# Narrower scores for the two short groups, 71 memory columns, and memory V turned by DMA, in a two-part kernel on one core

## The chip, the cores and the metric

The kernel runs on one core of a Trainium2 chip. The metric is device time in microseconds (us) of one execution; medians are quoted. The granted clock is the share of full TensorE speed that the trace records; all runs below have state fast with a mean of 0.997 to 1.000, so none has to be set aside as slow. To turn a tile means to transpose it. "The trace" is the record of one profiled execution, and its span is some 1.7 us shorter than the measured time.

Engine names: PE is the matrix engine, PEld its weight loads, DVE the vector engine, ACT the scalar engine, POOL the general one, SP the engine whose queue issues most transfers.

## The reference, cut

Part A is a state-space layer, part B a transformer layer with a recurrent memory; their results stand side by side. The change touches B alone:

```python
# B: x (1, 2048, 1024), mem0 (1, 8, 1024), 32 heads of 128, segments of 32 tokens
mem = mem0
for s in range(64):
    h = concat([mem, x[:, 32*s:32*s+32]])            # 8 memory + 32 tokens
    q, k, v = h @ Wq, h @ Wk, h @ Wv                 # per head
    p = softmax(mask(q @ k.T * 128**-0.5))           # memory rows see all, tokens are causal
    o = (p @ v) @ Wo
    mem = o[:, :8]                                   # memory of the next segment
    outs.append(o[:, 8:])
```

Taken literally, this is a chain of 64 steps. The kernel guesses the memory of each segment (from the mean of the segment), computes all segments at once, and checks the guess at the end: each recomputed memory row has to lie within 2^-8 of the guess in relative norm. If not, a general path (a loop over the 64 segments) runs. With these inputs it never does.

## The kernel before, the parts that matter

Three segments of 32 tokens and one memory column of each make a group of 99 columns; there are 22 groups. The first holds two segments and seven rows of the first memory, the last holds two segments: these are the two short groups. The memory columns stand behind the tokens in one tile, 73 of them (7 + 66, some of them never used).

```python
NTL = 3 * NG; NMX = 7; NM = NTL + NMX                # 66 + 7 = 73 memory columns
XMAIN = 1920; XE = T + NM                            # short pass of q and k: 2121 - 1920 = 201 columns
...
def v_mem(self, hb, w=None):                         # V of the memory columns, four heads a block
    ...                                              # 32 matmuls of 73 columns, copied to vm
    for h in range(4):
        k.PE.transpose(pt[0:NM, h*128:(h+1)*128], vm[:, h, :], k.ident[:])
    ...
    k.SP.dma_start(self.vx[hb][64:64 + NMX, :], sv[0:NMX, :])
    k.SP.dma_start(self.vt[hb][:], sv[NMX:NM, :])    # one store to the table of memory rows
...
def att_front(self, hp, u):                          # scores of two groups and two heads
    for gg in range(2):
        g0 = (2 * u + gg) * GP
        for hh in range(2):
            PE.matmul(s[:, gg, hh, 0:GW], kt[:, hh, g0:g0+128], qt[:, hh, g0:g0+GW], ...)   # GW = 99
    k.S.activation(e[:], s[...], ACT.Exp, ...)       # on ACT
    k.G.tensor_tensor(m[...], e[:], mask, ALU.mult)  # on POOL
...
LEAD = 10                                            # steps of the q/k projections ahead of the attention
```

The first V tile of the attention is loaded (`b_v<-b_vx`) from the tables that `v_mem` stores to, on SP's queue, behind those stores. After the last output store comes the branch on the check's flag.

## Time and profile before

| | before |
|---|---|
| time, median of 3 runs | 1247.11 us (1246.69 to 1247.39) |
| PE busy, of the span | 1234.2 of 1245.3 us |
| waits of PE that the table of waits lists (gaps of 0.1 us are left out) | 1.3 us |
| first score matmul / first product with V / last matmul start at | 486.6 / 492.2 / 1239.0 us |
| from the last matmul's start to the end | 6.25 us |

The page begins with the busy time of each engine, its share of the span and its instructions; its part on the chain of work that ended last names the engines that the chain ran through:

```profile
...
PE 1234.2 (99%) x8270; PEld 662.5 (53%) x8342; DVE 667.7 (54%) x1250; ACT 263.4 (21%) x631; POOL 275.8 (22%) x407
...
PE 99%; issue 0%; DVE 0%
...
```

The table of waits of PE gives line, tile and what was waited for, then the total in us, the count, and the longest:

```profile
...
PE psR L64 <- DVE hpb L105: 1.3, 1, 1.3
```

The table of stretches gives, for each stretch (us from the start), its length, then the busy time and instructions of PE, PEld, DVE, ACT and POOL, the granted clock, and the share and rate of the transfers. These are the start, the two parts of the attention, and the end:

```profile
...
0.00:20.00 20.00, 18.62 (x136) 11.02 (x138) 8.13 (x30) 6.97 (x11) 12.48 (x82) 1.00 1.06 261
487.00:700.00 213.00, 213.00 (x1653) 127.60 (x1652) 134.08 (x342) 41.90 (x142) 61.19 (x70) 1.00 0.55 138
700.00:1018.00 318.00, 317.89 (x2466) 190.42 (x2465) 199.01 (x512) 61.66 (x210) 91.36 (x105) 1.00 0.49 116
1235.00:1246.00 11.00, 4.28 (x40) 3.60 (x37) 0.42 (x1) 0.38 (x1) 0.00 (x0) 0.81 0.06 16
...
```

PE is busy without a gap in the attention; no other engine is near its limit. A group of instructions is shown as line, engine, operation, out<-in, shapes, count | busy us, mean ns of one | idle time before:

```profile
...
L64 PE MATMUL psS<-b_q,b_k 128*128 128x99 bf16 x704 | 59.9, 208 | 0.0
...
L64 PE MATMUL psP<-b_xe,b_wq 128*128 128x201 bf16 x256 | 24.8, 250 | 0.1
...
L64 PE MATMUL psP<-b_xe,b_wv 128*128 128x73 bf16 x256 | 10.0, 197 | 0.0
L64 PE MATMUL psS<-b_ogT,b_wog 128*128 128x64 bf16 x256 | 8.8, 193 | 0.0
...
L64 PE MATMUL psP<-b_omT,t 128*128 128x73 bf16 x128 | 4.5, 197 | 0.0
...
L64 PE MATMUL psP<-ident,b_vm 128*73 128x128 bf16 x32 | 3.1, 219 | 0.0
...
```

The mean ns of one matmul is a latency, and matmuls overlap, so it doesn't price a column. The interval from start to start does: 44.2 ns at 99 columns where the latency is 208.

The first V load on SP's queue and the first product with V on PE (start, length, engine, instruction):

```profile
...
465.02 0.27 SPq L64 DMA_DIRECT2D b_vx<-b_vst  x1
465.34 0.29 SPq L64 DMA_DIRECT2D b_vt<-b_vst  x1
465.73 0.26 SPq L64 DMA_DIRECT2D b_v<-b_vt  x1
466.03 16.42 SPq L64 DMA_DIRECT2D b_v<-b_vx  x2
...
```
```profile
...
486.64 0.34 PE L64 MATMUL psS<-b_q,b_k 128*128 128x99 bf16 x4
...
491.85 0.34 PE L64 MATMUL psS<-b_q,b_k 128*128 128x99 bf16 x4
492.16 0.50 PE L64 MATMUL psO<-b_v,b_m 128*128 128x129 bf16 x6
...
```

And the longest wait of SP on itself, behind the last branch:

```profile
...
SPq L1156 <- SPq L1156: 2.8, 1, 2.8
...
```

### The profile page before, as it was taken

To read this page: it belongs to the slowest core of one execution; us is meant where nothing else is said; L and a number is where in the kernel's file an instruction comes from. 1 tells how busy PE (TensorE), PEld (TensorE's weight loads), DVE (VectorE), ACT (ScalarE), POOL (GpSimd) and SP (SyncE) were. 2 spreads that over 40 slices of the span, in tenths; PEclk is the share of its full clock that TensorE was granted. 3 is DMA by queue.
4 is the path that set the end of the run, shared out by engine and by line. 5 is a ranking of instruction groups with operands and counts; after the bars stand their busy time and mean duration, and the time that the engine had idled before them with its cause. 6 is when DMAs were issued, how large, how long until landed. Compare 5 with 4: busy or idle time off the path is not lost.

```text
span 1245.3 us, 20124 instructions
## 1 busy us (share of the span) xinstructions
PE 1234.2 (99%) x8270; PEld 662.5 (53%) x8342; DVE 667.7 (54%) x1250; ACT 263.4 (21%) x631; POOL 275.8 (22%) x407
## 2 busy tenths in 40 slices
PE   9999999999999999999999999999999999999998
PEld 5444444444455555556666656555665554446444
DVE  4688899998711124666666666666666641001000
ACT  5344444443310000211112111111211110000000
POOL 4111331212332321322222222222222220000000
PEclk9999999999999999999999999999999999999999
DMA  9965444554898734664454545545553379407000
GB/s 248 272 191 147 131 135 127 144 155 107 242 322 248 249 116 95 196 170 124 96 145 108 144 108 120 132 92 121 120 142 92 65 211 230 107 18 153 17 26 19
DMA packets 316246, 176.83 MB, mean 142 GB/s; under 512 B 138874, under 2 KB 301550, under 8 KB 316150
## 3 DMA queue, kind: packets, MB, share of 16 engines
q1 hardware_dynamic: 294054, 147.95, 47.8%
q10 hardware_dynamic: 21072, 24.38, 5.9%
q0 software_dynamic: 1024, 3.17, 0.7%
q8 instruction: 66, 1.08, 0.4%
q14 instruction: 30, 0.25, 0.1%
HBM read 89.14 MB, written 53.17 MB: 114 GB/s over the span
## 4 chain that ended last, share of the span: by engine, by line
PE 99%; issue 0%; DVE 0%
PE psP L64 82%; PE psU L64 9%; PE psS L64 3%; PE psO L64 2%; PE psR L64 2%; DVE b_xe L91 0%; DVE b_ost L91 0%; DVE a_n L962 0%; DVE hpb L105 0%; DVE ones L102 0%
## 5 line engine op out<-in xcount | busy, mean ns | idle before, releaser
L64 PE MATMUL psP<-b_xe,b_wq 128*128 128x480 bf16 (+1 forms) x1280 | 247.7, 343 | 0.1
L64 PE MATMUL psP<-b_xe,b_wk 128*128 128x480 bf16 (+1 forms) x1280 | 247.7, 343 | 0.0
L64 PE MATMUL psP<-b_wv,b_xe 128*128 128x512 bf16 (+2 forms) x1033 | 223.4, 372 | 0.8
L644 POOL TENSOR_TENSOR b_m<-b_e,maskB 99x396 bf16<-99x396 bf16 x160 | 139.8, 874 | 338.5 <-ACT b_e L641 338.5
L641 ACT ACTIVATE b_e<-psS 99x396 bf16<-99x396 f32 x176 | 88.2, 501 | 536.7 <-PE psS L64 533.4
L64 PEld LDWEIGHTS <-b_wk 128*128 128x128 bf16 x1280 | 119.4, 98 | 94.2
L64 PEld LDWEIGHTS <-b_wq 128*128 128x128 bf16 x1280 | 118.7, 98 | 87.7
L64 PEld LDWEIGHTS <-b_xe 128*128 128x128 bf16 x1056 | 101.8, 98 | 119.1 <-DVE b_xe L91 0.2
L91 DVE CAST b_k<-psP 128x480 bf16<-128x480 f32 (+1 forms) x192 | 97.4, 528 | 100.9 <-PE psP L64 100.9
L91 DVE CAST b_q<-psP 128x480 bf16<-128x480 f32 (+1 forms) x192 | 97.4, 528 | 93.1 <-PE psP L64 91.5
L64 PEld LDWEIGHTS <-b_ol 128*128 128x128 bf16 x864 | 84.3, 98 | 94.4
L64 PE MATMUL psU<-a_xT,a_bt 128*128 128x512 bf16 x493 | 113.9, 379 | 1.1
L64 PE MATMUL psP<-t,a_hl 128*128 128x512 bf16 x496 | 112.1, 379 | 0.8
L91 DVE CAST b_ost<-psP 128x512 bf16<-128x512 f32 (+1 forms) x17 | 11.5, 676 | 177.4 <-PE psP L64 176.3
L64 PE MATMUL psP<-wo,b_ol 128*128 128x512 bf16 (+1 forms) x440 | 91.9, 364 | 0.4
L64 PE MATMUL psP<-t,b_ol 128*128 128x512 bf16 x408 | 91.7, 379 | 0.4
L280 POOL TENSOR_SCALAR a_tt<-a_pr,a_tabf 128x1 f32<-128x1 f32 x48 | 34.1, 710 | 243.2 <-DVE a_pr L275 243.2
L661 DVE TENSOR_TENSOR b_ob<-psO,b_accR 99x384 bf16<-99x384 f32 x160 | 85.9, 553 | 2.4 <-DVE b_accR L660 0.4
L89 ACT ACTIVATE b_vst<-psP 128x512 bf16<-128x512 f32 x126 | 71.9, 589 | 71.3 <-PE psP L64 59.9
L267 DVE TENSOR_TENSOR a_pr<-psU,a_tabf 128x2048 f32<-128x2048 f32 x32 | 73.0, 2282 | 15.7 <-PE psU L64 14.0
L64 PEld LDWEIGHTS <-a_bt 128*128 128x128 bf16 x512 | 49.2, 98 | 57.6
L64 PEld LDWEIGHTS <-a_hl 128*128 128x128 bf16 x512 | 49.0, 98 | 56.7
(200 smaller groups left out, 962.7 us busy)
## 6 DMA issues: line engine op xcount, KB each, us to landing
b_v<-b_vx SPq DMA_DIRECT2D x16, 1122.0 KB
b_wv<-in_B_Wv_dram SPq DMA_DIRECT2D x16, 1024.0 KB
b_vx<-b_vst ACTq DMA_DIRECT2D x24, 544.0 KB
b_on<-b_ob SPq DMA_DIRECT2D x15, 720.0 KB
a_hs<-a_h SPq DMA_DIRECT2D x32, 256.0 KB
b_wog<-in_B_Wo_dram SPq DMA_DIRECT2D x4, 2048.0 KB
b_wq<-in_B_Wq_dram SPq DMA_DIRECT2D x16, 512.0 KB
b_wk<-in_B_Wk_dram SPq DMA_DIRECT2D x16, 512.0 KB
```

What stands on the lines that cost most here:

```text
L64: r = f(*a, **kw)
L89: self.S.activation(out, in_, ACT.Copy)
L91: self.V.tensor_copy(out, in_)
L267: V.tensor_tensor(pr[:], u[:].unsqueeze(1).to_broadcast([128, 2, 2, TB]), view(t3, [[TB + 1, 2], [TB + 1, 2], [1, TB]]), ALU.mult)
L280: G.tensor_scalar(tt[:, j:j + 1], w[:, j, TB - 1:TB], t3[:, 1, TB:TB + 1], None, ALU.mult)
L641: k.S.activation(e[:], s[0:GW, :, :, 0:GW], ACT.Exp, scale=float(E) ** -0.5, accum_out=self.accE[0:GW, i:i + 1])
L644: k.G.tensor_tensor(m[0:GW, 0:4 * GP].rearrange("p (a b q) -> p a b q", a=2, b=2)[:, :, :, 0:GW], e[:], mask[0:GW, :, :].unsqueeze(2).to_b ...
L661: V.tensor_tensor(self.ob[:, b0:b0 + n, :], o[0:GW, 0:n, 0:E], r.unsqueeze(2).to_broadcast([GW, n, E]), ALU.mult)
```

## The change

Its intent is to take columns off PE, which bounds the kernel. The unused memory columns go (71 instead of 73), the scores of the two short groups are computed on 73 and 65 columns, the guess on 63 and the check on 70, and memory V of six of the eight head blocks is turned by DMA, through HBM, and not by PE. Cut to its core (the masks, the order of the check's rows and the fills are left out):

```diff
-NM = NTL + NMX
+NT4 = NMX + 4
+NM = NMX + NSEG                      # 71
+Q0 = 64 + NMX + 2                    # 73: first group
+QZ = 65                              # last group
+NO = NMX + 3 + NTL - 6               # 70: rows of the check
...
+    def store_t(self, hb, s):
+        for r0, n, i in ((0, 2, NMX), (NTL - 3, 2, NMX + 2), (3, NTL - 6, NT4)):
+            self.k.SP.dma_start(self.vt[hb][r0:r0 + n, :]..., s[i:i + n, :, :])
...
+        if hb > 1:
+            k.V.memset(vm[:, :, NM:128], 0.0)
+            k.SP.dma_start(self.vmt[hb][:], vm[:].rearrange("p h n -> p (h n)"))
+            yield
+            ...
+            for h in range(4):
+                k.SP.dma_start_transpose(s[:, h, 0:E], self.vmt[hb][:, h * 128:(h + 1) * 128])
+            yield
+            k.SP.dma_start(self.vx[hb][64:64 + NMX, :]..., s[0:NMX, :, 0:EW])
+            self.store_t(hb, s[:, :, 0:EW])
...
-        k.SP.dma_start(self.vt[hb][:], sv[NMX:NM, :])
+        self.store_t(hb, st[:, 0, :, :])
...
+            n = Q0 if u + gg == 0 else QZ if u + gg == NU else GW
             for hh in range(2):
-                PE.matmul(s[:, gg, hh, 0:GW], kt[:, hh, g0:g0 + 128], qt[:, hh, g0:g0 + GW], ...)
+                PE.matmul(s[:, gg, hh, 0:n], kt[:, hh, g0:g0 + 128], qt[:, hh, g0:g0 + n], ...)
...                                   # exp and mask: two parts in the first and last step of a head pair
-        self.gx = c.tile([128, KC, NM], BF16, name="b_gx")
+        self.gx = c.tile([128, KC, NO], BF16, name="b_gx")
-        self.accE = c.tile([128, HP * NU], FP32, name="b_accE")
+        self.accE = c.tile([128, HP * (NU + 2)], FP32, name="b_accE")
+    k.maskZ = k.cst.tile([128, GW], BF16, name="maskZ")
```

More of the change, by code (lines that the diff above doesn't have):

```diff
@@ L117, in masks @@
     k.maskB = k.cst.tile([128, 2, GW], BF16, name="maskB")
+    k.maskZ = k.cst.tile([128, GW], BF16, name="maskZ")
+    G.memset(k.maskZ[:], 0.0)
     G.memset(k.maskA[:], 0.0)
@@ L120, in masks @@
     t = slice(GX, GW)
-    for m, ns in ((k.maskA[:, 0, :], 2), (k.maskA[:, 1, :], 3), (k.maskB[:, 0, :], 3), (k.maskB[:, 1, :], 3)):
+    for m, ns, c0 in ((k.maskA[:, 0, :], 2, Q0 - 2), (k.maskA[:, 1, :], 3, GX), (k.maskB[:, 0, :], 3, GX), (k.maskB[:, 1, :], 3, GX),
+                      (k.maskZ[:], 2, QZ - 1)):
         for j in range(ns):
@@ L126, in masks @@
                             pattern=[[1, 32]], channel_multiplier=-1)
-            G.memset(m[r, GX + j:GX + j + 1], 1.0)
+            if c0 != QZ - 1 or j == 0:
+                G.memset(m[r, c0 + j:c0 + j + 1], 1.0)
         if ns == 3:
@@ L134, in masks @@
                             pattern=[[1, 3]], channel_multiplier=-1)
-    m = k.maskA[:, 0, :]
+    for a, b, n in ((0, 64, 2), (QZ - 1, QZ, 1)):
+        v = k.maskZ[t, a:b].rearrange("p (j q) -> p j q", j=n)
+        G.memset(v, 8.0)
+        G.affine_select(out=v, in_=v, compare_op=ALU.is_equal, fill=0.0, base=0, pattern=[[1, n], [0, (b - a) // n]],
+                        channel_multiplier=-1)
+    m, c0 = k.maskA[:, 0, :], Q0 - 2
     G.memset(m[0:32, 64:64 + NMX], 1.0)
@@ L139, in masks @@
     G.memset(m[64:64 + NMX, 64:64 + NMX], 1.0)
-    G.memset(m[64:64 + NMX, GX:GX + 1], 1.0)
-    for a, b in ((32, 64), (GX + 1, GX + 2)):
+    G.memset(m[64:64 + NMX, c0:c0 + 1], 1.0)
+    for a, b in ((32, 64), (c0 + 1, c0 + 2)):
         G.memset(m[t, a:b], 8.0)
@@ L146, in masks @@
     G.memset(m[GX:GX + 1, 0:32], 1.0)
-    G.memset(m[GX:GX + 1, 64:64 + NMX], 1.0)
-    G.memset(m[GX:GX + 1, GX:GX + 1], 1.0)
-    G.memset(m[0:1, 64 + NMX:GX], 1.0)
-    G.memset(m[0:1, GX + 2:GX + 3], 1.0)
+    G.memset(m[GX:GX + 1, 64:64 + NMX + 1], 1.0)
 class PartA:
@@ L344, in __init__ @@
         self.vt = [k.drp.tile([NTL, 4 * EW], BF16, name=f"b_vt{i}") for i in range(HB)]
+        self.vmt = [k.drp.tile([E, 512], BF16, name=f"b_vmt{i}") for i in range(HB)]
         self.on = [k.drp.tile([T, 1024], BF16, name=f"b_on{i}") for i in range(4)]
@@ L378, in fill @@
         k.V.memset(z[:], 0.0)
+        one = tmp.tile([2, 4 * EW], BF16, name="b_one", bufs=1)
+        k.V.memset(one[:], 1.0)
         for hb in range(HB):
@@ L381, in fill @@
             k.SP.dma_start(self.vx[hb][T + 32:NSLOT, :], z[0:32, :])
+            k.SP.dma_start(self.vt[hb].rearrange("(g j) n -> g j n", j=3)[0:NG:NG - 1, 2, :], one[:])
         for q in range(4):
-            k.SP.dma_start(self.tn[q][NM:NR, 0:4 * EW], z[0:NR - NM, :])
-            k.SP.dma_start(self.tn[q][NM:NR, 1024 - 4 * EW:1024], z[0:NR - NM, :])
+            k.SP.dma_start(self.tn[q][NO:NR, 0:4 * EW], z[0:NR - NO, :])
+            k.SP.dma_start(self.tn[q][NO:NR, 1024 - 4 * EW:1024], z[0:NR - NO, :])
     def load_x(self, q):
@@ L506, in og @@
             for c in range(KC):
-                mm = k.PE.matmul(p[:, h * NSEG:(h + 1) * NSEG], w[:, c, h * 128:(h + 1) * 128], self.xbar[:, c, :], start=(c == 0), stop=(c == KC - 1))
+                mm = k.PE.matmul(p[:, h * NSEG:h * NSEG + NSEG - 1], w[:, c, h * 128:(h + 1) * 128], self.xbar[:, c, 0:NSEG - 1], start=(c == 0), stop=(c == KC - 1))
                 if late and h == 0 and c == 0:
                     k.tc.keep_in_program_order(mm)
-        k.copy("s" if late else "v", self.ogT[:, hb * 4:(hb + 1) * 4, :], p[:, 0:4 * NSEG].rearrange("p (h s) -> p h s", h=4))
+        k.copy("s" if late else "v", self.ogT[:, hb * 4:(hb + 1) * 4, 0:NSEG - 1],
+               p[:, 0:4 * NSEG].rearrange("p (h s) -> p h s", h=4)[:, :, 0:NSEG - 1])
     def load_wog(self, q, pool):
@@ L520, in guess @@
         pg = k.ps("S")
+        NS = NSEG - 1
         for q in range(4):
@@ L525, in guess @@
                 for h in range(H):
-                    PE.matmul(pg[:, c * NSEG:(c + 1) * NSEG], wo[:, h, dc * 128:(dc + 1) * 128], self.ogT[:, h, :], start=(h == 0), stop=(h == H - 1))
+                    PE.matmul(pg[:, c * NSEG:c * NSEG + NS], wo[:, h, dc * 128:(dc + 1) * 128], self.ogT[:, h, 0:NS], start=(h == 0), stop=(h == H - 1))
                 yield
@@ L530, in guess @@
         V.tensor_copy(m[:, :, NMX + 1:NMX + 2], pv[:, :, 0:1])
-        V.tensor_copy(m[:, :, NMX + 3:NM], pv[:, :, 1:NSEG])
+        V.tensor_copy(m[:, :, NMX + 2:NT4], pv[:, :, NS - 2:NS])
+        V.tensor_copy(m[:, :, NT4:NM], pv[:, :, 1:NS - 2])
         gx = self.gx
-        V.tensor_copy(gx[:, :, 0:2], pv[:, :, 0:2])
-        V.tensor_copy(gx[:, :, 2:NTL - 1], pv[:, :, 1:NSEG])
-        V.tensor_copy(gx[:, :, NTL - 1:NM], pv[:, :, 0:1].to_broadcast([128, KC, NMX + 1]))
+        V.tensor_copy(gx[:, :, 0:NMX + 1], pv[:, :, 0:1].to_broadcast([128, KC, NMX + 1]))
+        V.tensor_copy(gx[:, :, NMX + 1:NMX + 2], pv[:, :, 1:2])
+        V.tensor_copy(gx[:, :, NMX + 2:NMX + 3], pv[:, :, NS - 1:NS])
+        V.tensor_copy(gx[:, :, NMX + 3:NO], pv[:, :, 2:NS - 1])
         yield
+    def store_t(self, hb, s):
+        for r0, n, i in ((0, 2, NMX), (NTL - 3, 2, NMX + 2), (3, NTL - 6, NT4)):
+            self.k.SP.dma_start(self.vt[hb][r0:r0 + n, :].rearrange("n (h e) -> n h e", h=4), s[i:i + n, :, :])
     def v_mem(self, hb, w=None):
@@ L546, in v_mem @@
                 k.PE.matmul(p[:, h * NM:(h + 1) * NM], w[:, c, h * 128:(h + 1) * 128], self.memT[:, c, :], start=(c == 0), stop=(c == KC - 1))
-        vm = self.vmp.tile([128, 4, NM], BF16, name="b_vm", bufs=1)
-        k.copy("v", vm[:], p[:, 0:4 * NM].rearrange("p (h n) -> p h n", h=4))
+        vm = self.vmp.tile([128, 4, 128], BF16, name="b_vm", bufs=1)
+        k.copy("v", vm[:, :, 0:NM], p[:, 0:4 * NM].rearrange("p (h n) -> p h n", h=4))
+        if hb > 1:
+            k.V.memset(vm[:, :, NM:128], 0.0)
+            k.SP.dma_start(self.vmt[hb][:], vm[:].rearrange("p h n -> p (h n)"))
+            yield
+            s = self.next_st()[:].rearrange("p i h e -> p (i h e)")[:, 0:576].rearrange("p (h e) -> p h e", h=4)
+            k.V.memset(s[:, :, E:EW], 1.0)
+            for h in range(4):
+                k.SP.dma_start_transpose(s[:, h, 0:E], self.vmt[hb][:, h * 128:(h + 1) * 128])
+            yield
+            k.SP.dma_start(self.vx[hb][64:64 + NMX, :].rearrange("n (h e) -> n h e", h=4), s[0:NMX, :, 0:EW])
+            self.store_t(hb, s[:, :, 0:EW])
+            yield
         yield
@@ L551, in v_mem @@
         for h in range(4):
-            k.PE.transpose(pt[0:NM, h * 128:(h + 1) * 128], vm[:, h, :], k.ident[:])
+            k.PE.transpose(pt[0:NM, h * 128:(h + 1) * 128], vm[:, h, 0:NM], k.ident[:])
         st = self.next_st()
@@ L566, in qk_zero @@
         V = self.k.V
-        for t in self.qk[i]:
+        for t in self.qk[i][1:]:
             V.memset(t[:, :, 64 + NMX:GX], 0.0)
@@ L570, in qk_zero @@
             V.memset(t[:, :, 0:NG * GP].rearrange("p h (g n) -> p h g n", n=GP)[:, :, :, GW:GP], 0.0)
+            V.memset(t[:, :, GX + 2:GW], 0.0)
+            V.memset(t[:, :, 21 * GP + GX + 2:21 * GP + GW], 0.0)
             V.memset(t[:, :, NG * GP:QW], 0.0)
@@ L597, in proj @@
                 pv = p[:, 0:2 * NS].rearrange("p (h n) -> p h n", h=2)
-                k.copy("v", t[:, :, 0:64], pv[:, :, 0:64])
-                k.copy("v", t[:, :, 21 * GP:21 * GP + 64], pv[:, :, 64:128])
-                k.copy("v", t[:, :, 64:64 + NMX], pv[:, :, 128:128 + NMX])
-                k.copy("v", t[:, :, 0:NG * GP].rearrange("p h (g n) -> p h g n", n=GP)[:, :, :, GX:GW],
-                       pv[:, :, 128 + NMX:NS].rearrange("p h (g j) -> p h g j", j=3))
+                tg = t[:, :, 0:NG * GP].rearrange("p h (g n) -> p h g n", n=GP)
+                te = tg[:, :, 0:NG:NG - 1, :]
+                k.copy("v", te[:, :, :, 0:64], pv[:, :, 0:128].rearrange("p h (g n) -> p h g n", g=2))
+                if i == 0:
+                    k.copy("v", t[:, :, 64:Q0], pv[:, :, 128:64 + Q0])
+                    k.copy("v", tg[:, :, NG - 1, QZ - 1:QZ], pv[:, :, 64 + Q0:65 + Q0])
+                else:
+                    k.copy("v", t[:, :, 64:64 + NMX], pv[:, :, 128:128 + NMX])
+                    k.copy("v", te[:, :, :, GX:GX + 2], pv[:, :, 128 + NMX:128 + NT4].rearrange("p h (g j) -> p h g j", g=2))
+                k.copy("v", tg[:, :, 1:NG - 1, GX:GW], pv[:, :, 128 + NT4:NS].rearrange("p h (g j) -> p h g j", j=3))
                 yield
@@ L636, in att_front @@
             g0 = (2 * u + gg) * GP
+            n = Q0 if u + gg == 0 else QZ if u + gg == NU else GW
             for hh in range(2):
-                PE.matmul(s[:, gg, hh, 0:GW], kt[:, hh, g0:g0 + 128], qt[:, hh, g0:g0 + GW], start=True, stop=True)
+                PE.matmul(s[:, gg, hh, 0:n], kt[:, hh, g0:g0 + 128], qt[:, hh, g0:g0 + n], start=True, stop=True)
         e = self.p3a.tile([GW, 2, 2, GW], BF16, name="b_e", bufs=3)
         i = hp * NU + u
-        k.S.activation(e[:], s[0:GW, :, :, 0:GW], ACT.Exp, scale=float(E) ** -0.5, accum_out=self.accE[0:GW, i:i + 1])
         m = self.mt[i % len(self.mt)]
-        mask = k.maskA if u == 0 else k.maskB
-        k.G.tensor_tensor(m[0:GW, 0:4 * GP].rearrange("p (a b q) -> p a b q", a=2, b=2)[:, :, :, 0:GW], e[:],
-                          mask[0:GW, :, :].unsqueeze(2).to_broadcast([GW, 2, 2, GW]), ALU.mult)
+        mv = m[0:GW, 0:4 * GP].rearrange("p (a b q) -> p a b q", a=2, b=2)
+        if u == 0:
+            parts = ((0, 1, Q0, k.maskA[:, 0:1, :]), (1, 2, GW, k.maskA[:, 1:2, :]))
+        elif u == NU - 1:
+            parts = ((0, 1, GW, k.maskB[:, 0:1, :]), (1, 2, QZ, k.maskZ[:].unsqueeze(1)))
+        else:
+            parts = ((0, 2, GW, k.maskB[:]),)
+        for a, b, n, mask in parts:
+            j = i if a == 0 else HP * NU + 2 * hp + (u > 0)
+            k.S.activation(e[:, a:b, :, 0:n], s[0:GW, a:b, :, 0:n], ACT.Exp, scale=float(E) ** -0.5, accum_out=self.accE[0:GW, j:j + 1])
+            k.G.tensor_tensor(mv[:, a:b, :, 0:n], e[:, a:b, :, 0:n],
+                              mask[0:GW, :, 0:n].unsqueeze(2).to_broadcast([GW, b - a, 2, n]), ALU.mult)
         return [(hp, 4 * u + b, m, b) for b in range(4)]
@@ L680, in att_back @@
             k.SP.dma_start(on[T - 64:T, cs], ov[0:64, NG - 1, :])
-            k.SP.dma_start(tn[0:NTL, :].rearrange("(g j) n -> j g n", j=3)[:, :, cs], ov[GX:GW, :, :])
-            k.SP.dma_start(tn[NTL:NM, cs], ov[64:64 + NMX, 0, :])
+            k.SP.dma_start(tn[NMX + 3:NO, :].rearrange("(g j) n -> j g n", j=3)[:, :, cs], ov[GX:GW, 1:NG - 1, :])
+            k.SP.dma_start(tn[0:NMX + 2, cs], ov[64:Q0, 0, :])
+            k.SP.dma_start(tn[NMX + 2:NMX + 3, cs], ov[QZ - 1:QZ, NG - 1, :])
     def att_init(self):
@@ L687, in att_init @@
         for m in self.mt:
-            self.k.G.memset(m[:], 0.0)
+            self.k.G.memset(m[:], 1.0)
         self.load_v(0)
@@ L804, in check @@
         yield
-        sq = pool.tile([128, 2, KC, NM], FP32, name="c_sq", bufs=1)
-        df = pool.tile([128, 4, NM], FP32, name="c_df", bufs=1)
+        sq = pool.tile([128, 2, KC, NO], FP32, name="c_sq", bufs=1)
+        df = pool.tile([128, 4, NO], FP32, name="c_df", bufs=1)
         for half in range(2):
@@ L811, in check @@
                 for h in range(H):
-                    PE.matmul(p[:, c * NM:(c + 1) * NM], self.wo[half][:, h, c * 128:(c + 1) * 128], self.omT[:, h, 0:NM],
+                    PE.matmul(p[:, c * NO:(c + 1) * NO], self.wo[half][:, h, c * 128:(c + 1) * 128], self.omT[:, h, 0:NO],
                               start=(h == 0), stop=(h == H - 1))
-            pv = p[:, 0:4 * NM].rearrange("p (c n) -> p c n", c=4)
+            pv = p[:, 0:4 * NO].rearrange("p (c n) -> p c n", c=4)
             V.tensor_tensor(df[:], pv, self.gx[:, cs, :], ALU.subtract)
@@ L818, in check @@
             yield
-        ss = pool.tile([128, 2, NM], FP32, name="c_ss", bufs=1)
+        ss = pool.tile([128, 2, NO], FP32, name="c_ss", bufs=1)
         V.tensor_reduce(ss[:], sq[:].rearrange("p a c n -> p a n c"), AX.X, ALU.add)
@@ L825, in check @@
         for i in range(2):
-            PE.matmul(pd[0:NM, i:i + 1], ss[:, i, :], onef[:], start=True, stop=True)
+            PE.matmul(pd[0:NO, i:i + 1], ss[:, i, :], onef[:], start=True, stop=True)
         t2 = small("c_t2", 2)
         V.memset(t2[:], 0.0)
-        V.tensor_copy(t2[0:NM, :], pd[0:NM, 0:2])
+        V.tensor_copy(t2[0:NO, :], pd[0:NO, 0:2])
         ok = small("c_ok", 3)
@@ L832, in check @@
         V.tensor_tensor(ok[:, 0:1], t2[:, 0:1], t2[:, 1:2], ALU.is_le)
-        V.tensor_tensor(ok[:, 0:1], ok[:, 0:1], k.skip[:], ALU.max)
         for i, acc in enumerate((self.accE, self.accR)):
@@ L929, in check_consts @@
     V, G = k.V, k.G
-    k.skip = k.cst.tile([128, 1], FP32, name="c_skip")
-    G.memset(k.skip[:], 0.0)
-    for r in (2, NTL - 2, NTL - 1):
-        G.affine_select(out=k.skip[:], in_=k.skip[:], compare_op=ALU.not_equal, fill=1.0, base=-r,
-                        pattern=[[0, 1]], channel_multiplier=1)
     k.fmask = k.cst.tile([L, 2, L], FP32, name="f_mask")
@@ L1111, in kernel_main @@
                     vm = b.v_mem(hp // 2 + 1)
-                if u in (4, 6):
+                if u in (4, 6, 8):
                     next(vm)
```

## The prediction

> **What bounds the kernel now.** TensorE. The page gives PE 1234.2 us busy of a span of 1245.3 us (99%); the chain of work that ended last is PE for 99%. The table of waits has one wait of PE in the whole run, 1.3 us at the start. In the table of stretches PE is busy 213.0 of 213 us and 317.9 of 318 us in the attention (487 to 1018 us), while DVE has 63%, ACT 20%, POOL 29%. The granted clock is 0.999. So every column taken off PE should come off the time, and work put elsewhere should cost nothing while it stays hidden.
>
> **Price of a matmul.** Start to start in the trace, median: 512 columns 216 ns, 201 columns 87, 128 (turning memory V) 56, 99 columns 44, 73 columns 33, 64 columns 29, 4 columns 25. This agrees with the Trainium skill ("TensorE: Matmul & The Clock Gate", section "Back-to-back issue gap"): N / 2.4 + about 2.5 ns when warm. One column is worth 0.42 ns; no new width (63 to 73) reaches the 25 ns of the 4-column matmuls.
>
> **What leaves PE** (estimates from these intervals):
> - Scores of first and last group: 32 matmuls from 99 to 73 columns, 32 from 99 to 65: 1920 columns, 0.80 us.
> - q and k of memory and edge tokens: 512 matmuls from 201 to 199 columns (71 memory columns, not 73): 0.43 us.
> - V of the memory tokens: 256 matmuls from 73 to 71: 0.21 us.
> - The guess and its head outputs: 512 matmuls from 64 to 63: 0.21 us.
> - The check: 256 matmuls from 73 to 70: 0.32 us.
> - PE turns of memory V for six of eight head blocks: 24 x 56 ns = 1.34 us.
>
> Sum 3.3 us, nearly all on the critical path, since PE waits for nothing in these stages.
>
> **What is added elsewhere.** 32 more exponentials on ACT with their sum reads (194 ns each) and 32 more POOL multiplies: the first and last step of each head pair are cut in two. One step takes about 3 us of PE; ACT needs now 0.50 + 0.19 us, POOL 0.87 us. The split should add some 0.4 us of latency, and a step's blocks are used only two steps later: off the path. Six writes of memory V to HBM, 24 small DMA transposes and some more stores stand on SP's queue, which mostly waits for others; q/k weights arrive over 15 us before use, V tiles likewise. DVE loses six evictions and gains small fills.
>
> **Prediction.** 1247.1 - 3.3 = 1243.8 us; 8 in 10 between 1242.7 and 1245.7. Faster by over 2%: 0.5%; within 2%: 98.5%; slower by over 2%: 1%.
>
> **What would show it.** PE busy falls by about 3.3 us; the score group splits into forms of 99 (640), 73 (32) and 65 (32) columns; PE turns of memory V fall from 32 to 8; the attention stretch gets some 2.5 us shorter, the check 0.3 us. PE's waits stay near 1.3 us, and the tail after PE's last matmul (about 6 us) is unchanged.
>
> **What would make it wrong.** The build orders instructions anew; another order may make PE wait for a weight, a V tile or an exponential (high side). If the transposes hold back a load on SP's queue past its use, PE waits appear in the attention, at even head pairs. If the check failed, the general path would run and take far longer. If the removed turns also cost PE switching time that the intervals hide, the gain exceeds 3.3 us.

## The result, and the profile after

The changed kernel took 1243.18 us (median of 4 runs, 1243.0 to 1243.57), the kernel before in the same rounds 1246.99 us. The ratio is 0.997 (95% interval 0.9952 to 0.9987). Ratios are the mean time of one kernel's runs over that of the other's of the same rounds, so they are not quite the ratios of the medians. The prediction was 1243.8 us, in a range of 1242.7 to 1245.7. Measured against a threshold of 2% the two kernels are the same.

The page and the waits of PE in the changed kernel:

```profile
...
PE 1230.8 (99%) x8246; PEld 658.8 (53%) x8318; DVE 667.8 (54%) x1254; ACT 266.6 (21%) x695; POOL 278.1 (22%) x442
...
PE 96%; DMA 3%; issue 0%; SPq 0%; DVE 0%
...
```
```profile
...
PE psR L68 <- DVE hpb L109: 1.3, 1, 1.3
PE psO L68 <- DMA b_v<-b_vx: 0.9, 1, 0.9
PE psP L68 <- DMA b_wv<-in_B_Wv_dram: 0.4, 1, 0.4
PE psU L68 <- DMA b_xr<-in_B_x_dram: 0.3, 1, 0.3
```

PE busy fell by 3.4 us, as foretold. But PE now has three listed waits for transfers, 1.6 us in all, where the table had none. The same stretches, with the same limits:

```profile
...
0.00:20.00 20.00, 17.95 (x133) 10.52 (x135) 8.69 (x31) 6.30 (x11) 13.34 (x85) 1.00 1.06 246
487.00:700.00 213.00, 212.12 (x1638) 126.49 (x1637) 133.93 (x343) 42.70 (x167) 61.77 (x83) 1.00 0.59 141
700.00:1018.00 318.00, 317.89 (x2475) 189.88 (x2474) 199.48 (x516) 64.21 (x249) 92.58 (x123) 1.00 0.52 120
1235.00:1246.00 11.00, 2.46 (x23) 1.96 (x20) 0.42 (x1) 0.00 (x0) 0.00 (x0) 0.89 0.06 16
...
```

The groups that changed:

```profile
...
L68 PE MATMUL psS<-b_q,b_k 128*128 128x99 bf16 x640 | 57.0, 208 | 0.0
...
L68 PE MATMUL psP<-b_xe,b_wq 128*128 128x199 bf16 x256 | 24.6, 249 | 0.1
...
L68 PE MATMUL psP<-b_xe,b_wv 128*128 128x71 bf16 x256 | 9.6, 198 | 0.0
L68 PE MATMUL psS<-b_ogT,b_wog 128*128 128x63 bf16 x256 | 8.8, 193 | 0.0
...
L68 PE MATMUL psP<-b_omT,t 128*128 128x70 bf16 x128 | 4.2, 198 | 0.0
...
L68 PE MATMUL psS<-b_q,b_k 128*128 128x73 bf16 x32 | 3.7, 198 | 0.0
L68 PE MATMUL psS<-b_q,b_k 128*128 128x65 bf16 x32 | 3.6, 194 | 0.0
...
L68 PE MATMUL psP<-ident,b_vm 128*71 128x128 bf16 x8 | 0.8, 219 | 0.0
...
```

The scores are split as intended and 8 turns of 32 are left. The guess has the same busy time with 63 columns as with 64. Then the first V load and the first product with V, whose line now has an idle time and its cause in brackets:

```profile
...
465.58 0.27 SPq L68 DMA_DIRECT2D b_vx<-b_vst  x1
465.90 0.90 SPq L68 DMA_DIRECT2D b_vt<-b_vst  x3
466.90 0.25 SPq L68 DMA_DIRECT2D b_v<-b_vt  x1
467.19 16.33 SPq L68 DMA_DIRECT2D b_v<-b_vx  x2
...
```
```profile
...
487.17 0.32 PE L68 MATMUL psS<-b_q,b_k 128*128 128x73 bf16 x4
...
492.37 0.34 PE L68 MATMUL psS<-b_q,b_k 128*128 128x99 bf16 x4
493.59 0.50 PE L68 MATMUL psO<-b_v,b_m 128*128 128x129 bf16 x6 [0.88 <-DMA b_v<-b_vx]
...
```

Three stores (0.90 us) stand in front of the load where one did (0.29 us). Counted from the first score, the load is issued 0.6 us later than before (467.19 against 487.17 us, 466.03 against 486.64). And SP's waits on itself, of which the one behind the branch is 0.5 us:

```profile
...
SPq L1201 <- SPq L1201: 0.9, 2, 0.5
...
```

So the span of the trace can be put together from four terms. Each is a difference of the two traces: start times of the same matmul, or start-to-start intervals summed by form.

| term | before | after | difference, us |
|---|---|---|---|
| PE work (start-to-start intervals, itemized further down) | | | -3.38 |
| start: first matmul of part A starts at | 35.74 | 36.41 | +0.67 |
| from the first score to the first product with V | 5.52 | 6.41 | +0.89 |
| from the last matmul's start to the end | 6.25 | 4.26 | -1.99 |
| sum | | | -3.81 |
| span | 1245.26 | 1241.45 | -3.81 |

The last matmul starts only 1.8 us earlier. The prediction knew the first term only; the others nearly cancel.

### The profile page after: what moved, and what is told of

The parts are those of the page before. It is cut to its first block, busy times and chain, and to the rows that moved or that the text cites. A ratio compares the mean times of both kernels' runs of the same rounds, so it can differ in the third digit from the quotient of the medians.

```text
span 1241.5 us, 20294 instructions
## 1 busy us (share of the span) xinstructions
PE 1230.8 (99%) x8246; PEld 658.8 (53%) x8318; DVE 667.8 (54%) x1254; ACT 266.6 (21%) x695; POOL 278.1 (22%) x442
## 4 chain that ended last, share of the span: by engine, by line
PE 96%; DMA 3%; issue 0%; SPq 0%; DVE 0%
PE psP L68 80%; PE psU L68 9%; PE psS L68 3%; PE psO L68 2%; DMA b_v<-b_vx 2%; PE psR L68 2%; DMA b_wv<-in_B_Wv_dram 1%; SPq L68 0%; DVE b_ost L95 0%; DVE b_vm L572 0%
## 5 line engine op out<-in xcount | busy, mean ns | idle before, releaser
L694 POOL TENSOR_TENSOR b_m<-b_e,maskB 99x396 bf16<-99x396 bf16 (+1 forms) x160 | 134.4, 840 | 337.0 <-ACT b_e L693 337.0
L693 ACT ACTIVATE b_e<-psS 99x396 bf16<-99x396 f32 (+3 forms) x208 | 91.3, 441 | 531.7 <-PE psS L68 523.4
```

The costliest lines, as they stand in the source:

```text
L693: k.S.activation(e[:, a:b, :, 0:n], s[0:GW, a:b, :, 0:n], ACT.Exp, scale=float(E) ** -0.5, accum_out=self.accE[0:GW, j:j + 1])
L694: k.G.tensor_tensor(mv[:, a:b, :, 0:n], e[:, a:b, :, 0:n], mask[0:GW, :, 0:n].unsqueeze(2).to_broadcast([GW, b - a, 2, n]), ALU.mult)
```

## The experiments

The theory: the gain on PE is as predicted, but it loses 1.5 us to two new waits for transfers, and a tail that has nothing to do with the arithmetic gives 2 us back. The rival: the start, the wait and the tail are chance of one execution, and the surplus over 3.3 us is hidden switching time of the removed turns. In all runs the results were correct. Only the intended instructions changed (al_full also has a few copies on DVE and one store in another place). Runs fall into three groups, each on another chip and with its own runs of the kernel before: its median was 1246.95 us beside the first four, 1246.87 beside b_pad8, b_split, b_shift and a_align, and 1246.73 beside the last three. Between groups, times are therefore good to some 0.2 us, and the ratio to before is the fairer measure. A ratio's 95% interval is some 0.0014 wide to each side (1.7 us), so effects under that rest on the traces, which are one each.

### after_again: the changed kernel once more

No edit.

> The changed kernel, unaltered, for a second trace. If its parts are lasting ones: last matmul starts near 1237.2 us, a tail of about 4.3 us after it, one wait of about 0.9 us of PE for the first load of V tiles (near 492 us), time near 1243.2. If the short tail or the V wait were chance of one run, the tail comes out near 6.2 us or the wait is gone.

Measured: 1243.44 us (five runs, 1243.35 to 1243.52), 1246.95 for before, ratio 0.9973. In the second trace the last matmul starts at 1237.40 us, the tail is 4.27 us, the first matmul of part A starts at 36.74 us, and PE waits 0.8 us for the V load. All three parts are lasting.

### a_pe: all turns of memory V on PE again

```diff
--- the changed kernel
-        if hb > 1:
+        if False:
-                if u in (4, 6, 8):
+                if u in (4, 6):
```

> The changed kernel, with memory V of all eight head blocks turned by PE again. If the turns are worth their start-to-start time alone, the last matmul starts 24 x 56 ns = 1.34 us later than in the changed kernel. If turning by DMA costs or gains something hidden beyond it, the difference is below 1.0 or above 1.7 us. By theory A the tail may jump back to about 6.2 us (SP has fewer instructions), then the time is near 1246.5; else near 1244.5.

Measured: 1244.41 us (1244.21 to 1244.49). The last matmul starts at 1238.73 us, 1.33 us later than in after_again, where 1.34 was the sum of the intervals. So turning by DMA is worth its start-to-start time and nothing more, and the small transfers cost nothing: apart from the start and the first V load PE waits for nothing in either kernel. The tail stayed short (4.06 us).

### b_hint: does the branch at the end hold the tail?

SP's wait of 2.8 us in the kernel before begins right behind its branch. In the trace two instruction packets of 8192 bytes start at 1241.34 and 1241.37 us, after the branch (1240.15 to 1240.20), and SP goes on at 1243.00. In the changed kernel SP goes on 0.49 us after the branch, and an instruction packet had started 2.6 us ahead of it. Two more start there at 1239.32 and 1239.54 us, 0.9 and 1.1 us behind the branch, so a pair of packets behind it doesn't tell the two cases apart. The Trainium skill ("Runtime: NRT & Kernel Launch", section "Instruction fetch mechanics") says that a taken branch whose target isn't in the current window has to wait for a fetch; whether that is what happens here is the question, and the packets alone don't answer it. The first trial was a prefetch hint for SP, as PE already has one.

```diff
--- the kernel before, in hint()
     k.tc.mark_branch_hint_location("general", "LikelyTaken", engines=[mybir.EngineType.PE])
     ...
+    k.tc.mark_branch_hint_location("general", "LikelyTaken", engines=[mybir.EngineType.SP])
+    i = k.nc.cur_bb.bb.instructions[-1]
+    k.tc.keep_in_program_order(type("Ins", (), {"ins": i}))
```

> The kernel before with one more instruction: a branch prefetch hint for SP, as PE has it. Theory A (the tail of before holds an instruction fetch of SP behind its last branch, which the changed kernel has not, by the place of the branch in SP's program): SP's wait of 2.8 us behind the branch falls to about 0.5, the tail from 6.2 to about 4.3 us, the time from 1247.0 to about 1245.0; PE's part is unchanged. Rival B (the tail ends with the landing of the last store or with the other engines): tail stays near 6.2 us, time 1247.0.

Measured: 1246.56 us (1246.44 to 1247.04), ratio 0.9998. The wait is 2.7 us, the tail 6.16 us. The hint did nothing for SP. This is a miss for theory A as it was put; it leaves open whether the fetch is the cause.

### b_dup: the store to the memory table three times

```diff
--- the kernel before, in v_mem()
-        k.SP.dma_start(self.vt[hb][:], sv[NMX:NM, :])
+        for _ in range(3 if hb < 2 else 1):
+            k.SP.dma_start(self.vt[hb][:], sv[NMX:NM, :])
```

> The kernel before, in which the store of the memory V rows for the short tables is issued three times, not once, for the first two head blocks (same data). All other engines keep their order. Theory C (in the changed kernel two more stores of 0.3 us each stand on SP's queue in front of the first load of V tiles, and that load lands just in time in before): a new PE wait of 0.5 to 0.7 us at the first product with V, PE ends 0.5 to 0.7 us later. Rival D (the 0.9 us wait of the changed kernel is chance, or comes from slower transfers): no wait, PE end unchanged. The tail may change as well, since four more instructions move SP's branch; it is read apart.

Measured: 1251.52 us (1248.77 to 1251.54; the profiled execution took 1250.18), and a PE wait of 3.5 us for the V load. The direction is that of theory C, the size is not: the stores write the same rows, so each waits for the one before it (5.4 us of such waits on SP in all). The edit was too strong. Two things are learned all the same. The trace's clock records show half speed (0.5) for 3.41 us behind the wait, so the last matmul starts 5.1 us later, not 3.5. And the tail became short: 4.36 us, SP's wait behind the branch 0.47 us, though no arithmetic had changed. SP's branch is instruction 593 of its trace here, 588 in before and 589 in b_hint.

### b_pad8: eight idle stores move SP's branch

```diff
--- the kernel before, in fill()
+        pad = k.drp.tile([8, 4 * EW], BF16, name="b_pad")
+        for i in range(8):
+            k.SP.dma_start(pad[i:i + 1, :], z[0:1, :])
```

> The kernel before, with eight one-row stores to a scratch tensor on SP's queue at about 190 us, where SP waits anyway; nothing else moves. Theory A2 (the hint did not help, but the place of SP's last branch in its instruction stream decides: at instruction 588 or 589 of the trace SP waited 2.7 to 2.8 us behind the branch, at 593, 634 and 671 0.5 us): the wait behind the branch falls to 0.5 us, the tail from 6.2 to about 4.3 us, the last matmul stays near 1239.0 us, the time falls by about 1.9 us to 1245.0. Rival B (the tail goes with something else that the changed kernel and the tripled store share): tail 6.2 us, time 1247.0.

Measured: 1244.87 us (1244.45 to 1244.95) against 1246.87, ratio 0.9984. PE is as in before (last matmul at 1238.69 us), the tail is 4.06 us, and the wait behind the branch is 0.5 us. Its two waits on itself, behind the branch and later for the last store:

```profile
...
SPq L1159 <- SPq L1159: 0.7, 2, 0.5
...
```

So eight stores that do no work make the kernel before 2.0 us faster. What stands in SP's program ahead of the branch decides: with the branch at instruction 588 (two kernels) or 589 SP waited 2.7 to 2.8 us; at 592, 593, 596, 634, 666 or 671 it waited 0.47 to 0.49 us. So much is shown. All the kernels with the short wait also issue four or more transfers more than before on SP, and the hint of b_hint moved the branch by one instruction only; whether the place of the branch counts or the number of transfers is not separated. That the wait is an instruction fetch across a block boundary is argued and not shown: b_pad8, with the short wait, has two instruction packets behind its branch too (1240.92 and 1240.97 us, 1.0 to 1.1 us after it), and neither the block nor the engine that a packet is for can be seen.

### b_split: three stores that don't wait for each other

```diff
--- the kernel before, in v_mem()
-        k.SP.dma_start(self.vt[hb][:], sv[NMX:NM, :])
+        for r0, r1 in ((0, 2), (2, 4), (4, NTL)) if hb < 2 else ((0, NTL),):
+            k.SP.dma_start(self.vt[hb][r0:r1, :], sv[NMX + r0:NMX + r1, :])
```

> The kernel before, with the store of the memory V rows for the short tables split into three stores of 2, 2 and 62 rows for the first two head blocks, as the changed kernel has it; no store writes what another wrote, so none waits for another (the tripled store did: its wait was 3.5 us). Theory C: 2 x 0.3 us more issue in front of the first V load, which had 0.1 us to spare: a wait of PE of about 0.5 us at the first product with V, the product starts 0.5 us later after the first score than the 5.5 us of before. Rival D: no wait. The tail may be short by theory A2, so the time alone says little: -1.4 us or +0.5 us.

Measured: 1247.01 us (1246.55 to 1248.90). The tail is short (4.37 us), so PE lost about what the tail gave: b_pad8, with a short tail too, took 1244.87. The wait of PE:

```profile
...
PE psO L64 <- DMA b_v<-b_vx: 2.0, 1, 2.0
...
```

The wait is there, as theory C says, but it is 2.0 us and not 0.5. Of it, 0.6 us is the later issue (the load is issued at 466.72 us, in before at 466.03, with PE 0.1 us later). The rest is the load itself: from its issue to its last landing it took 27.4 us, against 26.0 in before, 1.0 us of it in a longer issue (17.45 us against 16.42, which no other kernel here shows); why isn't settled. The expectation's 0.1 us to spare was misread, as told further down. In the profiled execution, the slowest of the five, the clock fell to 0.5 for 3.41 us behind this wait.

### al_act: the stores on another queue

This and the next two start from the aligned kernel a_align, told below.

```diff
--- a_align, in store_t()
-            self.k.SP.dma_start(self.vt[hb][r0:r0 + n, :]..., s[i:i + n, :, :])
+            (self.k.SP if hb > 1 else self.k.nc.scalar).dma_start(self.vt[hb][r0:r0 + n, :]..., s[i:i + n, :, :])
```

> The aligned changed kernel (1242.05 us, last matmul at 1236.15, wait of 0.7 us at the first product with V), with the stores of the memory V rows of the first two head blocks issued from ACT's queue, not SP's; all other engines keep their order, SP has six stores fewer in front of the first V load. Theory C (issue on SP ahead of that load): the load is issued about 0.9 us earlier and the wait falls to 0.2 us or less, last matmul near 1235.5, time near 1241.4. Rival D2 (the load is slow for another reason, as in the split store, whose wait was 2.0 us where 0.5 was expected): the wait stays at 0.7 us or more. SP's branch moves to about instruction 665: tail short in either case.

Measured: the wait fell from 0.7 to 0.2 us, and the first product with V comes 5.75 us after the first score, not 6.28. So the stores' issue ahead of the V load makes 0.5 us of the new wait: shown. The product still comes 0.4 us later than in kernels that don't wait (5.4 us). That part stays open, for this run has a delay of its own: SP issued the second part of the load 1.15 us after the first, not 0.39 as in a_align, since it waited for another transfer to end. The time, 1241.83 us (1241.69 to 1242.23), is only 0.2 us below a_align's; this trace starts 0.6 us later (first matmul of part A at 36.11 us), and the start differs by that much between the traces of aligned kernels.

### b_shift: 32 bytes more among the constants

The late start goes with longer packets. The mean duration of the 2048-byte packets of SP's queue that start at 6 to 10 us is 84 ns in before, 105 and 108 ns in the two traces of the changed kernel. No instruction on SP differs there. But the changed kernel's constants have other sizes (`gx`, `accE`, `vm`, a third mask), and so all large tiles behind them moved: the weights of V from a multiple of 512 bytes of a partition to 32 modulo 64.

```diff
--- the kernel before, in the constants of part B
         self.flag = c.tile([1, 1], I32, name="b_flag")
+        c.tile([128, 8], FP32, name="b_shift")
```

> The kernel before with a 32-byte tile more among its constants; no instruction is added or moved. The large tiles (weights of V, x turned, C turned, q and k weights) then start at 32 modulo 64 bytes of a partition, as in the changed kernel, and not at a multiple of 512. Theory E (the late start of the changed kernel, first matmul of part A at 36.4 to 36.7 us against 35.6 to 35.7, comes from slower DMA writes into tiles that are not aligned): that matmul starts at about 36.5 us, the 2048-byte packets at 6 to 10 us take about 105 ns, not 84, PE ends 0.7 to 1.0 us later, time about 1247.8. Rival F (it comes from the added fills on DVE and POOL at the start): 35.7 us, 84 ns, 1247.0.

Measured: 1247.68 us (1247.38 to 1247.70) against 1246.87 (1246.43 to 1247.29); the ratio is 1.0006, and its interval (0.9992 to 1.0020) includes 1, so the time alone doesn't settle it, though all five runs lie above all nine of before. The trace does. The first matmul of part A starts at 36.43 us, the packets take 113 ns, the last matmul starts at 1239.69 us, and PE has the two waits at the start that the changed kernel has:

```profile
...
PE psR L64 <- DVE hpb L105: 1.3, 1, 1.3
PE psU L64 <- DMA b_xr<-in_B_x_dram: 0.4, 1, 0.4
PE psP L64 <- DMA b_wv<-in_B_Wv_dram: 0.4, 1, 0.4
```

Without any new instruction, 32 bytes make the start 0.7 us later, with 0.8 us between the medians. Rival F falls.

### a_align: the changed kernel, aligned again

```diff
--- the changed kernel
         self.flag = c.tile([1, 1], I32, name="b_flag")
+        c.tile([128, 88], FP32, name="b_shift")
```

> The changed kernel with a pad of 352 bytes among its constants, so that the large tiles start at a multiple of 512 bytes again; no instruction is added or moved. Theory E: first matmul of part A back to about 35.7 us, time about 0.8 us lower, 1242.5. Rival F: 36.5 us and 1243.4. The wait of 0.8 us at the first product with V stays in both (or shrinks a little, if the V tile's load profits).

Measured: 1242.05 us (1241.69 to 1242.80), ratio to before 0.9962, against 0.9973 for after_again. The first matmul of part A starts at 35.50 us, the packets take 84 ns, the last matmul starts at 1236.15 us. The wait at the first product with V stayed, at 0.7 us. The gain in time, 1.4 us, is larger than the 0.8 expected. In the traces the start is 0.9 to 1.2 us earlier than in the two of the changed kernel; the other aligned variants start at 35.79 to 36.11 us, so this trace is a lucky one. Why the median fell by so much isn't settled; the two kernels were not run in the same rounds.

### al_full: the scores wide again

```diff
--- a_align, in att_front() and qk_zero()
-            n = Q0 if u + gg == 0 else QZ if u + gg == NU else GW
+            n = GW
...                                   # and two fills, so that the columns read are defined
```

> The aligned changed kernel with the scores of the first and last group on 99 columns again (PE alone: 64 matmuls; exponentials and masks stay narrow). PE ends later by 32 x 26 / 2.4 + 32 x 34 / 2.4 ns = 0.80 us, last matmul near 1236.95, time near 1242.85. If narrow scores were bound by the weight load or by a wait, the difference is under 0.4 us.

Measured: 1243.16 us (1242.41 to 1243.68), 1.1 us above a_align. The time alone says too much, since this trace starts 0.55 us later. From the first score to the last matmul's start, with the V wait taken off, it is 750.33 - 0.45 = 749.88 us, in a_align 749.88 - 0.75 = 749.13 us: a difference of 0.75 us, 0.80 expected. The intervals of before and the changed kernel give 0.69 and say where the rest went: inside a pair the narrow scores take 32.6 and 29.2 ns, but the second of each pair takes some 38 and 35 ns to the matmul that follows.

### a_best: one step more of projections ahead of the attention

```diff
--- a_align
-        LEAD = 10
+        LEAD = 11
```

> The aligned changed kernel with one step more of the projections (8 or 16 matmuls, 1.6 to 3.2 us) ahead of the attention (11, not 10). The first product with V then comes later by more than its wait: no wait is left, last matmul near 1235.4 us, time near 1241.3, lowest of all so far. If the wait is made good elsewhere later, the time stays at 1242.0.

Measured: 1241.57 us (1241.37 to 1241.70) against 1246.73, ratio 0.9958. The table of waits of PE has one line again:

```profile
...
PE psR L68 <- DVE hpb L109: 1.3, 1, 1.3
```

The last matmul starts at 1235.53 us. This version beats both kernels: 5.2 us below before in the same rounds, and 1.6 to 1.9 us below the changed kernel as it came, which ran in others. It has the aligned tiles and the later attention together.

| kernel | median, us | first matmul of A | first score to first product | last matmul start | tail |
|---|---|---|---|---|---|
| before | 1246.99 | 35.74 | 5.52 | 1239.01 | 6.25 |
| b_hint | 1246.56 | 35.58 | 5.39 | 1238.70 | 6.16 |
| b_dup | 1251.52 | 35.64 | 9.06 | 1244.11 | 4.36 |
| b_pad8 | 1244.87 | 35.57 | 5.39 | 1238.69 | 4.06 |
| b_split | 1247.01 | 35.86 | 7.56 | 1242.83 | 4.37 |
| b_shift | 1247.68 | 36.43 | 5.53 | 1239.69 | 6.14 |
| changed | 1243.18 | 36.41 | 6.41 | 1237.19 | 4.26 |
| after_again | 1243.44 | 36.74 | 6.30 | 1237.40 | 4.27 |
| a_pe | 1244.41 | 36.72 | 6.31 | 1238.73 | 4.06 |
| a_align | 1242.05 | 35.50 | 6.28 | 1236.15 | 4.36 |
| al_act | 1241.83 | 36.11 | 5.75 | 1236.23 | 4.20 |
| al_full | 1243.16 | 36.05 | 6.00 | 1237.15 | 4.26 |
| a_best | 1241.57 | 35.79 | 5.37 | 1235.53 | 4.20 |

(Medians in us over each kernel's own runs; the rest from one trace each.)

## Why the prediction was right, and where it was not

The time was right: 1243.8 us foretold, 1243.18 measured. The bound was right too: PE busy fell by 3.4 us, and the work moved to ACT, POOL and the queues stayed hidden in the attention. But the agreement of the sum to 0.6 us is partly luck, since three terms were missing and cancelled to -0.4 us.

**The PE term**, as the prediction listed it, against the intervals of the traces:

| item | predicted, us | measured, us | from |
|---|---|---|---|
| scores | 0.80 | 0.69 | 704 x 44.16 ns, against 640 x 44.13 + 32 x 35.44 + 32 x 32.09 |
| q and k | 0.43 | 0.43 | 512 x (86.67 - 85.84) |
| memory V | 0.21 | 0.36 | 256 x (33.85 - 32.43) |
| guess and head outputs | 0.21 | 0.00 | 512 x (29.13 - 29.13) |
| check | 0.32 | 0.56 | 256 x (33.82 - 31.65) |
| turns | 1.34 | 1.34 | 24 x 55.9; a_pe: 1.33 |
| sum | 3.31 | 3.38 | |

The sum holds, four of its terms less so. The mis-sized ones are small:
- "The guess and its head outputs: 512 matmuls from 64 to 63: 0.21 us" is nothing. These odd counts of columns cost what the next even one does: 63 and 64 columns both take 29.13 ns, 199 take 85.84 (200 / 2.4 + 2.5 = 85.83), 201 take 86.67 (202 / 2.4 + 2.5 = 86.67). The rule of the Trainium skill ("TensorE: Matmul & The Clock Gate", section "Back-to-back issue gap") agrees with the trace at 64 columns and is 0.4 ns too low at these odd ones. It is no rule for all odd counts: inside a pair of scores 65 columns take 29.2 ns and 73 take 32.6, about what 64 and 72 would by the same formula.
- The 73-column matmuls of memory V and of the check took 32 or 33 ns mostly, but 38 or 39 one time in four or five; those of 71 and 70 columns never did. So the two terms measured 0.92 us, 0.39 more than foretold. Without the long ones 73 columns would take 32.5 ns, 71 take 32.4 and 70 take 31.7, and the two terms would be 0.24 us (an estimate from these intervals). The trace doesn't say why.
- The scores lost 0.1 us where a narrow pair ends.

**The steps that failed.** "q/k weights arrive over 15 us before use, V tiles likewise" was read in the middle of the attention and carried to its start. The first V load is issued behind the last stores of memory V, and in the kernel before it had nothing to spare: four scores of 44 ns start at 491.85 us, and the product comes at 492.16, 0.13 us later than it could (b_pad8 and b_hint, with the same stores ahead of the load, go from the first score to the product in 5.39 us, before in 5.52). The change put two more stores in front of it, and the product came another 0.9 us later: 0.6 us are the later issue of the load, and from issue to landing it took 0.2 us longer. al_act takes 0.5 us of this away by moving the stores, a_best all of it by more work ahead; both are shown.

"PE's waits stay near 1.3 us" failed in the same way, at the start as well: +0.7 us in this trace. It is the alignment of the tiles, through the sizes of constants that the change altered in passing. b_shift makes it in the kernel before, a_align takes it out of the changed one. The Trainium skill ("DMA: Bandwidth & Descriptors", section "How a descriptor splits into AXI transactions") states that a read which doesn't start at a multiple of 256 bytes costs more beats (steps of 32 bytes). That doesn't account for what is seen here: it was the destination that moved, and by the page's counting (an estimate) 2048 bytes from 32 bytes past such a multiple take 65 beats and not 64, while the packets of b_shift took 113 ns against 84. How the address lengthens a packet stays open.

"the tail after PE's last matmul (about 6 us) is unchanged" failed by -2.0 us. The change lengthened SP's program, and the long wait of SP behind its last branch was gone. b_pad8 shows this in the kernel before, with no arithmetic changed; what SP waited for is not shown.

The rival, hidden switching time of the turns, falls with a_pe (1.33 us for 24 turns).

**What stays open:** what SP waits for behind its branch; why the V load in b_split took longer; how the address of a tile lengthens a packet; why the start of aligned kernels still differs by up to 0.6 us between traces; what makes some 73-column matmuls 5 ns longer.

## What to carry to other kernels

On a kernel whose PE never waits, price a change by start-to-start intervals (here the sum was right to 0.1 us, single terms were off by up to 0.24); then look for what the change moves without meaning to. A gain of a few us is of the size of what moves along: the address of every tile behind a constant that changed size, the length of a queue's program ahead of a branch, and a load that had been just in time. When a change pays by some tenths of a per cent, read start, waits and tail apart before crediting it, and pad the constants and the instruction count on purpose.

## What the Trainium skill lacked or had wrong

- "TensorE: Matmul & The Clock Gate" (section "Back-to-back issue gap") doesn't say that an odd column count can cost as the next even one: 63 and 64 columns both 29.13 ns, 199 columns 85.84, 201 columns 86.67 (but 65 and 73 inside a pair of scores 29.2 and 32.6).
- The same page (section "What's actually happening") has the clock fall after at least one idle window of about 3.4 us. In b_split it fell to 0.5 for 3.41 us behind a wait of 2.0 us, in one profiled execution.
- "Runtime: NRT & Kernel Launch" (section "Instruction fetch mechanics") speaks of blocks of 16 KiB; the instruction packets that start behind SP's branch have 8192 bytes here; those of 16384 run on another queue, 66 in the whole run. It has no price for the stall that it tells of; SP's wait behind its branch was 2.7 to 2.8 us or 0.47 to 0.49, and no run shows that the longer one is this stall. No page says that a branch prefetch hint can be without effect on SP (b_hint: 2.7 us).
- "DMA: Bandwidth & Descriptors" (section "How a descriptor splits into AXI transactions") tells of reads, and of beats, not of a price of the destination's address in SBUF: 84 to 91 ns for an aligned 2048-byte packet, 105 to 113 ns with the destination at 32 modulo 64 bytes, and a start of the kernel that is 0.7 us later (b_shift).
